# A fused attention and expert kernel: the first expert's second layer as eight block products, small maxima in PSUM, and a new order

## The chip, the cores and the metric

The kernel runs on one core of one Trainium2 chip. A core has a matrix engine (TensorE, PE in the profile), a vector engine (VectorE, DVE), an activation engine (ScalarE, ACT), a third elementwise engine (GpSimd, POOL) and an engine that starts transfers (SyncE, SP). The engines run side by side, each through its own list of instructions in order, and wait for one another by semaphores. SBUF is the on-chip memory that all of them reach; PSUM holds the results of matmuls in banks of 512 fp32 columns. The metric is the device time of one execution in microseconds (us): the median of three runs of the kernel before is 576.9 us, the lowest 575.75, the highest 577.33.

## What is computed

Three parts follow each other. Attention of 2 batches x 8 heads over 576 positions (half of the heads see the last 32 positions, half every 32nd position); a layer h = max(x w1, x w2, x w3) w_out over the 1152 tokens; and four experts, each of two layers, summed with a weight for each token:

```python
for e in range(E):                       # E = 4
    h = np.maximum(x @ w1[e], 0.0)       # 1152 x 512 by 512 x 1024
    out += p[:, e:e + 1] * (h @ w2[e])   # 1152 x 1024 by 1024 x 512
```

All is fp32. The kernel gets that precision on TensorE from f16 pairs: every operand is scaled by a power of two and split into a high part hi (a rounding to f16) and a rest lo (what is left), and each product is three matmuls, hi hi, hi lo and lo hi.

## The kernel before

The tokens are worked in quarters i = 0 to 3 (256 tokens for i = 0, 2 and 320 for i = 1, 3). In the attention part, `att_a` makes the scores of one pair of heads in PSUM, takes the largest of each row (L315), subtracts it and exponentiates on ScalarE; `att_n` divides by the row sums; `att_t` transposes on TensorE and `att_p` multiplies with v and splits the result into the tile `x` (high part L404 on ScalarE, rest L405 on VectorE). The next product in the same bank `ops` waits until L405 has read the last one. Where SUB holds an 'o', the maximum is not subtracted but goes, times 0.125 (L319, a VectorE operation on 3 to 5 columns), as a bias into the exponential. Meanwhile the six blocks of w1, w2, w3 come in (`load_w`), are decoded (`decode64`: L200 to L216), scaled (`scale_w`) and split (`split_w`: L441 to L448). A scale needs the maximum over all partitions: `all_max` makes it with a small matmul into the tile `rows` and a VectorE reduction (L135), and `scale_of` turns it into a power of two with three more tiny VectorE operations (L146, L149, L140). `g1` (L410 to L412) is the first layer with its three-way maximum on VectorE (L467, L468), its high part on ScalarE (L469) and its rest on GpSimd (L470); `g2` is the w_out layer.

In the experts both layers are products of 2x2 blocks by the seven-product scheme: instead of eight block products, seven, of sums and differences of blocks. So `prep_w1` and `prep_w2` load the weights, take a scale (eight ScalarE passes, L164, `junk`), and split not only the four blocks but also three sums of them (`splits`: sums L577 to L582, high parts L171, rests L172). In `gemm1`, seven products of a unit leave PSUM through ScalarE copies (L662, L666, L670, L680 to L685) and VectorE additions (L673, L676, L679) into the tiles `c`; `finish` makes three more sums of the hidden blocks in `hsum` (a part of the tile `x2acc`; four additions, L692, L693, L699, L700) and splits two blocks and the three sums (L703 high parts on ScalarE, L704 rests). `gemm2` then makes seven products of 12 matmuls (L817) for each of four units of an expert, and adds each product into one or two quarters of the output with the token's weight (L847, for the first expert's first write of a quarter L845 on ScalarE); `gemm2_tail` does the last 128 tokens with four plain products. Matmuls wait for a free bank: five banks `w` and three banks `mm` (`e`), freed by these copies and additions.

The order: ORDER lists the steps up to the first expert by hand; the tables A0 to C1 say how many steps of weight preparation go with each unit of the experts; LATE and a scheduler that sorts by priority set the order inside an engine. The strings SUB, ACC, REB, WLO, LOP, TW and others choose the engine of single steps (d VectorE, p GpSimd, a ScalarE).

Of the kernel before, what the change touches and what calls it, by code (L numbers as in the profile page):

```python
# [8 lines left out]
F32 = mybir.dt.float32  # L9
# [17 lines left out]
SUB = 'ddoppdpppoooodoo'  # L27
ACC = 'bggbggggggggbgbg'
SGN = 'dddpppdp'
PTC = 'aaaaaaaaaaaaaada'  # L30
LOW = 'adaadaaa'
REB = 'adppppda'
WLO = 'qddqdd'
ARS = 'dpdp'
RB = 1
QB = 3
XS = [0, 0, 10]
W20 = [5, 0, 5, 0, 1, 2, 1, 1]
W10 = [0, 2, 3, 0, 4, 2, 2, 2]
W2S = [0, 1, 1, 0, 1, 0, 6, 5, 6, 0, 6, 3, 7, 0, 0, 1, 0]  # L40
W1S = [10, 1, 1, 4, 0, 16, 6, 6, 5, 0, 2, 2, 2, 3, 2, 8, 0]

ORDER = """
    lw0 lq02 lq01 lv01 aa02 lq00 lq03 aa01 wd0 lq20 lv00 lw1 lq21 lv21 aa00 aa03 lv20 an02 lq23 aa20 an00 wa0
    an20 an03 wd1 lw2 vs0 lq22 wd2 at00 ap00 aa22 at02 lq12 lq10 at20 an01 lv10 at01 lv11 wp0 aa21 lq11 lq13
    at03 an22 aa23 an23 wa1 an21 vs2 ap02 at21 aa12 an12 aa11 ap01 an11 at22 lw3 wa3 lq30 wd3 lq32 aa10 lw4 wa2
    an10 at11 ap03 ap21 ap22 vs1 wd4 at23 ap20 ap23 lq33 wp2 aa13 lq31 at10 at12 lw5 wp1 wa4 g00 lv31 aa30 aa31
    an13 wp3 g01 ap10 g20 lv30 vs3 an30 at13 ap12 g22 wp4 g21 g02 ap11 lo0 aa32 aa33 g03 wa5 g23 od0 wd5 an32
    oa0 at32 ap13 g10 lo1 od1 ap32 an33 oa1 at30 wp5 os op3 at33 ap33 ap30 op1 g14 g25 an31 op4 g24 at31 ap31 fo
    ew ew ew op0 op5 op2 ew g04 g05 go20 go21 go22 go00 ew ew g11 go03 go23 ew go02 g15 go01 g12 xw ew g30 ew xw  # L50
    g13 g32 go10 xw ew g35 go11 ew g34 xw ew xw g31 g33 go30 ew ew ew xw xw cl xw ew go12 ew xw go31 go33 go32
    go13 fw fw fw m yw fw yw yw yw fw fw yw yw yw m m m yw fw fw yw
"""
CB = 5
LATE = [1, 4]
A0 = [9, 4, 0, 0, 11, 4, 3, 15]
A1 = [5, 10, 6, 2, 2, 6, 1, 3]
B0 = [0, 4, 0, 3, 1, 6, 5, 4, 4, 7, 0, 0, 0]
B1 = [3, 0, 2, 0, 0, 0, 0, 1, 5, 7, 0, 4, 0]
C1 = [8, 10, 4, 0, 7, 2, 2, 0, 9, 2, 0, 0, 0]  # L60
LOP = 'pddpdpdddpdddddddddddddd'
SOP = 'dpdddddd'
TW = 'ddddddpd'
TW0 = 'dddd'
TLO = 'd'
WHI = 'aaadap'
# [6 lines left out]
def kernel(ctx, tc, qk0l, qk0s, qk1l, qk1s, vl, vs0, vs1, vn, masks, w123, wo, probs, we1, we2, out):  # L73
# [39 lines left out]
    def rows_tile():  # L113
        if "psw" in lay:
            return lay["psw"].tile([128, 512], F32, tag="w", name=nm("rows"))[:, :128]
        return psa.tile([128, 512], F32, tag="t", name=nm("rows"))[:, :128]
# [963 lines left out]
```

## Time and profile before

| what | value |
|---|---|
| median of the runs | 576.9 us (575.75 to 577.33) |
| the profiled execution | 576.31 us, of it 574.5 us span |
| TensorE busy | 542.7 us, 94% |
| VectorE busy | 445.0 us, 77% |
| ScalarE busy | 351.2 us, 61% |
| GpSimd busy | 126.7 us, 22% |
| matmuls | 4633 |

The span runs from the first to the last instruction; 1.8 us of the profiled execution lie around it. TensorE is busy nearly all the time after the first 80 us, so the time is its columns plus its waits, and a wait is found in the rows that name what ended an idle time (`<-` stands before the releaser). A matmul's row lasts longer than the distance to the next one, because matmuls overlap: an idle time in the rows is thus shorter than the time lost.

### The profile page before, as it was taken

The page shows a single profiled execution, that of the slowest core. Times are in us where ns is not written, and L with a number is a line of the kernel's source. Part 1 is how long each engine was busy: PE and PEld are TensorE (multiplying, and loading weights), DVE is VectorE, ACT ScalarE, POOL GpSimd, SP SyncE. Part 2 cuts the span into 40 slices and gives each one's busy share as a digit, 9 for nine tenths or more (in the row PEclk, how much of TensorE's full clock was granted, in tenths as well). Part 3 has the DMA queues.
Part 4 walks back from the last instruction along what each step waited for, and adds up shares of the span by engine and source line. Part 5 has one row for each costly group of instructions (what it writes and reads, how often), then busy time and mean ns, then how long its engine had stood idle before and what let it go on. Part 6 is the DMA issues. An engine that isn't in the chain of part 4 may idle for free.

```text
span 574.5 us, 11609 instructions
## 1 busy us (share of the span) xinstructions
PE 542.7 (94%) x4633; PEld 444.5 (77%) x4633; DVE 445.0 (77%) x835; ACT 351.2 (61%) x798; POOL 126.7 (22%) x108
## 2 busy tenths in 40 slices
PE   7779989999999999988999989999999999999997
PEld 4668768788777778766788867888767888867886
DVE  3999999752269524899998789899779999989732
ACT  3578556554446254998969888438697444776300
POOL 0467773710112112401020040010040010040000
PEclk9969999999999999999999999999999999999999
DMA  8998514124004000200425501444500331101342
GB/s 309 341 391 263 174 41 149 52 74 148 1 1 148 2 0 1 75 2 19 147 65 211 166 2 38 127 120 158 185 1 19 103 118 57 38 1 37 94 129 74
DMA packets 24150, 58.60 MB, mean 102 GB/s; under 512 B 3272, under 2 KB 3528, under 8 KB 23328
## 3 DMA queue, kind: packets, MB, share of 16 engines
q1 hardware_dynamic: 23952, 57.57, 30.7%
q8 instruction: 36, 0.59, 0.4%
q10 hardware_dynamic: 144, 0.30, 0.2%
q14 instruction: 18, 0.15, 0.1%
HBM read 48.42 MB, written 9.44 MB: 101 GB/s over the span
## 4 chain that ended last, share of the span: by engine, by line
PE 47%; DVE 19%; ACT 13%; DMA 10%; issue 10%; POOL 1%; SPq 0%; ACTq 0%; POOLq 0%; DVEq 0%
PE g L410 7%; PE g L412 7%; PE g L411 7%; PE e L817 7%; PE w L817 5%; DMA st<-in_we_dram 5%; ACT junk L164 3%; DMA v<-in_vs_dram 2%; DVE w1ops L172 2%; PE e L651 2%; PE e L653 2%; PE e L652 2%; ACT hb L703 2%; PE w L651 2%; PE ops L397 2%
## 5 line engine op out<-in xcount | busy, mean ns | idle before, releaser
L817 PEld LDWEIGHTS <-hb 128*128 128x128 f16 x1008 | 98.2, 98 | 17.3 <-issue 5.3
L410 PE MATMUL g<-x,w 128*128 128x256 f16 (+1 forms) x288 | 80.8, 287 | 3.1 <-DVE t L467 1.9
L412 PE MATMUL g<-x,w 128*128 128x256 f16 (+1 forms) x288 | 82.3, 287 | 0.0
L411 PE MATMUL g<-x,w 128*128 128x256 f16 (+1 forms) x288 | 82.3, 287 | 0.0
L651 PE MATMUL e<-xops,w1ops 128*128 128x320 f16 (+1 forms) x224 | 63.6, 287 | 6.4 <-ACT c L662 2.4
L651 PE MATMUL w<-xops,w1ops 128*128 128x256 f16 (+1 forms) x224 | 63.3, 284 | 2.6 <-ACT c L666 1.3
L652 PE MATMUL e<-xops,w1ops 128*128 128x320 f16 (+1 forms) x224 | 63.9, 287 | 0.0
L652 PE MATMUL w<-xops,w1ops 128*128 128x256 f16 (+1 forms) x224 | 63.5, 284 | 0.0
L653 PE MATMUL w<-xops,w1ops 128*128 128x256 f16 (+1 forms) x224 | 63.3, 284 | 0.0
L653 PE MATMUL e<-xops,w1ops 128*128 128x320 f16 (+1 forms) x224 | 63.2, 288 | 0.0
L652 PEld LDWEIGHTS <-w1ops 128*128 128x128 f16 x448 | 43.8, 98 | 22.9 <-issue 12.3
L653 PEld LDWEIGHTS <-w1ops 128*128 128x128 f16 x448 | 43.8, 98 | 10.9
L651 PEld LDWEIGHTS <-w1ops 128*128 128x128 f16 x448 | 43.8, 98 | 10.5
L470 POOL TENSOR_TENSOR h<-t,h 128x256 f16<-128x256 f32 (+1 forms) x24 | 21.7, 910 | 88.0 <-ACT h L469 82.2
L817 PE MATMUL e<-B,hb 128*128 128x256 f16 x288 | 35.0, 272 | 1.7 <-ACT c L684 1.6
L411 PEld LDWEIGHTS <-w 128*128 128x128 f16 x288 | 28.3, 98 | 9.9 <-issue 2.8
L410 PEld LDWEIGHTS <-w 128*128 128x128 f16 x288 | 28.3, 98 | 8.5 <-issue 0.9
L412 PEld LDWEIGHTS <-w 128*128 128x128 f16 x288 | 28.3, 98 | 7.2
L703 ACT CAST hb<-c 128x512 f16<-128x512 f32 x40 | 24.5, 620 | 12.2 <-DVE c L699 11.5
L704 DVE TENSOR_TENSOR hb<-x2acc,hb 128x768 f16<-128x768 f32 (+1 forms) x31 | 27.9, 904 | 4.5 <-ACT hb L703 4.3
L171 ACT ACTIVATE w1ops<-st,s 128x1024 f16<-128x1024 f32 x19 | 21.2, 1141 | 15.8 <-DVE st L582 5.5
L580 POOL TENSOR_TENSOR st<-st,x2acc 128x1024 f32<-128x1024 f32 x3 | 8.9, 2976 | 93.4 <-DVE x2acc L578 63.5
(229 smaller groups left out, 1383.8 us busy)
## 6 DMA issues: line engine op xcount, KB each, us to landing
st<-in_we_dram SPq DMA_DIRECT2D x10, 1024.0 KB, 5.5
st<-in_w_dram SPq DMA_DIRECT2D x6, 1536.0 KB, 8.0
c<-accd SPq DMA_DIRECT2D x24, 256.0 KB, 2.8
accd<-c SPq DMA_DIRECT2D x23, 256.0 KB, 2.0
st<-in_wo_dram SPq DMA_DIRECT2D x2, 1536.0 KB, 7.7
st<-in_we_dram SPq DMA_DIRECT2D x6, 512.0 KB, 4.5
x2acc<-in_we_dram SPq DMA_DIRECT2D x6, 512.0 KB, 4.1
qk<-in_qk1s_dram SPq DMA_DIRECT2D x4, 684.0 KB, 9.7
```

The costliest lines, as they stand in the source:

```text
L164: nc.scalar.activation(junk, src, AF.Abs, scale=2.0**-12, accum_out=dst)
L171: nc.scalar.activation(hi, src, AF.Copy, scale=s)
L410: nc.tensor.matmul(psum, lh, rh, start=i == 0, stop=False)
L411: nc.tensor.matmul(psum, lh, rl, start=False, stop=False)
L412: nc.tensor.matmul(psum, ll, rh, start=False, stop=i == n - 1)
L470: nc.gpsimd.tensor_tensor(hh[:, 1, fc, :], t1[:, :n], hh[:, 0, fc, :], ALU.subtract)
L651: nc.tensor.matmul(pt, wh, xh, start=first and k == 0, stop=False, skip_group_check=True)
L652: nc.tensor.matmul(pt, wh, xl, start=False, stop=False, skip_group_check=True)
L653: nc.tensor.matmul(pt, wl, xh, start=False, stop=k == 1, skip_group_check=True)
L703: nc.scalar.copy(hi, src)
L704: eng(LOP[8 * g + 4 * j + fp]).tensor_tensor(lo, src, hi, ALU.subtract)
L817: nc.tensor.matmul(pt, hop[:, x, f, sl], wop[:, y, f, :], start=start and n == 0, stop=n == 11, skip_group_check=True)
```

## The change

It does six things. First, for expert 0 alone the second layer is done with eight plain block products in place of seven: `finish` skips the sums of hidden blocks and splits two blocks instead of five, `prep_w2` splits the four weight blocks as they are, and `gemm2` accumulates each output quarter over two products in one bank and writes it out with a single ScalarE instruction. Second, the tile `rows` is kept whole and its columns 128 and 129 hold the maximum and the scale before rounding, so these small values lie in PSUM, not SBUF. Third, where SUB is 'o' the row maxima are written into columns 500 on of the score bank in PSUM, and L319's successor (L318) reads them there. Fourth, other engines: the small addition `ars` of quarters 1 and 2 goes to ScalarE, six of the 24 rests of `g1` from GpSimd to VectorE (HLO), two multiplications of the decoding from GpSimd to VectorE (REB), the split of block 5 of w1, w2, w3 to GpSimd (WLO), one sum of w2's blocks per later expert from GpSimd to VectorE (TW, at L580), one rest of the hidden blocks as well (LOP). Fifth, one more head pair subtracts its maximum (SUB), and three row sums change sides (ACC). Sixth, ORDER, A0 to C1 and LATE are new.

```diff
-SUB = 'ddoppdpppoooodoo'
-ACC = 'bggbggggggggbgbg'
+SUB = 'ddoppdpppoooodod'
+ACC = 'bgbbgggggbggbggg'
...
-REB = 'adppppda'
-WLO = 'qddqdd'
-ARS = 'dpdp'
+REB = 'addppdda'
+WLO = 'qddqdq'
+ARS = 'daad'
...
-    lw0 lq02 lq01 lv01 aa02 lq00 lq03 aa01 wd0 lq20 lv00 lw1 lq21 lv21 aa00 aa03 lv20 an02 lq23 aa20 an00 wa0
+    lw0 lq02 lq01 lv01 aa02 lq00 lq03 lq20 aa01 aa00 lq21 lv00 an02 aa03 lw1 wd0 wa0 wp0 lv20 lq23 lw2 lv21 wd1
...
-LATE = [1, 4]
-A0 = [9, 4, 0, 0, 11, 4, 3, 15]
+HLO = 'pdpdpppppppdpdpppdppppdp'
+LATE = [0, 0]
+A0 = [18, 12, 2, 0, 11, 2, 6, 14]
...
-LOP = 'pddpdpdddpdddddddddddddd'
+LOP = 'pddpdpdddddddddddddddddd'
-TW = 'ddddddpd'
+TW = 'dddddddd'
...
-            return lay["psw"].tile([128, 512], F32, tag="w", name=nm("rows"))[:, :128]
+            return lay["psw"].tile([128, 512], F32, tag="w", name=nm("rows"))
...
-        allr = sc.tile([128, 1], F32, tag="allr", name=nm("allr"))
-        nc.vector.tensor_reduce(allr, rows, AX.X, ALU.max)
+        allr, m = rows[:, 128:129], rows[:, 129:130]
+        nc.vector.tensor_reduce(allr, rows[:, :128], AX.X, ALU.max)
...
-            nc.vector.tensor_reduce(mx[:rows, gs], s3, AX.X, ALU.max, negate=True)
+            top_of = st[:rows, 500 : 500 + n] if SUB[4 * i + p] == "o" else mx[:rows, gs]
+            nc.vector.tensor_reduce(top_of, s3, AX.X, ALU.max, negate=True)
...
-                nc.vector.tensor_scalar(mx[:rows, gs], mx[:rows, gs], 0.125, None, ALU.mult)
+                nc.vector.tensor_scalar(mx[:rows, gs], top_of, 0.125, None, ALU.mult)
...
-        if ARS[i] == "p":
+        if ARS[i] == "a":
+            nc.scalar.activation(rs[:rows, :ng], sm[:rows, :ng], AF.Copy, bias=1e-9)
+        elif ARS[i] == "p":
...
-        nc.gpsimd.tensor_tensor(hh[:, 1, fc, :], t1[:, :n], hh[:, 0, fc, :], ALU.subtract)
+        eng(HLO[6 * i + fc]).tensor_tensor(hh[:, 1, fc, :], t1[:, :n], hh[:, 0, fc, :], ALU.subtract)
...
+        if e == 0:
+            for n, x in zip((1, 3, 2, 5), blocks):
+                yield from split1(op[n][:, 0], op[n][:, 1], x, s)
+            return
...
-                add(s[:, 0], m[1][:, 0], m[1][:, 1], ALU.add)
-                add(s[:, 1], s[:, 0], m[0][:, 0], ALU.subtract)
+                if e:
+                    add(s[:, 0], m[1][:, 0], m[1][:, 1], ALU.add)
+                    add(s[:, 1], s[:, 0], m[0][:, 0], ALU.subtract)
...
-                for g, (t, src) in enumerate(zip(hh, (m[0], m[1], s))):
+                for g, (t, src) in enumerate(zip(hh, (m[0], m[1], s) if e else m)):
...
+        if e == 0:
+
+            def part(b, z):
+                pt = bank(z == 1)
+                for n, (x, y) in enumerate(((1, (1, 3)), (2, (2, 5))) if b == 0 else ((3, (1, 3)), (6, (2, 5)))):
+                    mult(pt, h[x], w[y[z]], sl, n == 0, n == 1)
+                nc.scalar.activation(o[b][:, Z[z]], pt, AF.Copy, scale=k[b])
+                if z:
+                    nc.sync.dma_start(out=accd[:, 2 * j + q, 512 * b : 512 * b + 512], in_=o[b])
```

Three places show what moved. The first is VectorE's list at the first quarter's tile `x` (here `x_130`; `sps` are score banks, `amx` row maxima, `st` a weight block in decoding). Before:

```order
L315 TENSOR_REDUCE amx_323<-sps_325 128x4
...
L315 TENSOR_REDUCE amx_376<-sps_378 128x4
L319 TENSOR_SCALAR amx_323<-amx_323 128x4
L405 SCALAR_TENSOR_TENSOR x_130<-ops_311,s_295,x_130 128x256
L319 TENSOR_SCALAR amx_376<-amx_376 128x4
L216 SCALAR_TENSOR_TENSOR r_277<-st_1_72 128x1536
```

After the change, at the same place:

```order
L314 TENSOR_REDUCE sps_342<-sps_342 128x4
L126 TENSOR_REDUCE red_479<-vm_475 128x1
L318 TENSOR_SCALAR amx_340<-sps_342 128x4
L411 SCALAR_TENSOR_TENSOR x_130<-ops_328,s_282,x_130 128x256
L318 TENSOR_SCALAR amx_387<-sps_389 128x4
L214 SCALAR_TENSOR_TENSOR r_251<-st_1_72 128x1536
```

The sequence is the same, but the small multiplication takes its input from the score bank. The second place is VectorE's list some 35 us later, at a head pair of quarter 2 (`x_132` its tile, `h` the rests of `g1`). Before:

```order
L202 TENSOR_SCALAR st_0_71<-st_0_71 128x1536
L135 TENSOR_REDUCE allr_654<-rows_652 128x1
...
L315 TENSOR_REDUCE amx_830<-sps_832 128x5
L319 TENSOR_SCALAR amx_812<-amx_812 128x5
L149 TENSOR_SCALAR inv_657<-m_649 128x1
L329 TENSOR_TENSOR p_829<-sps_832,amx_830 128x480
```

After the change:

```order
L200 TENSOR_SCALAR st_0_71<-st_0_71 128x1536
L355 RECIPROCAL ar_915<-ars_913 120x6
L476 TENSOR_TENSOR h_713<-t_831,h_713 128x256
L314 TENSOR_REDUCE sps_766<-sps_766 128x5
L131 TENSOR_REDUCE rows_656<-rows_656 128x1
L318 TENSOR_SCALAR amx_764<-sps_766 128x5
L411 SCALAR_TENSOR_TENSOR x_132<-ops_679,s_487,x_132 128x256
```

A rest of `g1` (L476, both inputs in SBUF) now stands between the decoding step and the small multiplication. The third place is ScalarE's list where the first expert's second weights are split (`B` and `B2c` hold them; `e` and `w` are banks of the first layer). Before:

```order
L666 COPY c_2544<-w_3134 128x320
L171 ACTIVATE B_3093<-st_0_71,s_3091 128x1024
L171 ACTIVATE B2c<-st_1_72,s_3091 128x1024
L171 ACTIVATE B_3093<-st_1_72,s_3091 128x1024
L697 CAST tailh<-c_2545 128x2x64
L703 CAST hb_2534<-c_2545 128x2x256
L684 ACTIVATE c_2546<-e_2981 128x320
...
L171 ACTIVATE B2c<-st_0_71,s_3091 128x1024
```

After the change:

```order
L692 ACTIVATE c_2627<-e_2931 128x320
L169 ACTIVATE B_3035<-st_0_71,s_3033 128x1024
L169 ACTIVATE B_3036<-st_0_71,s_3033 128x1024
L169 ACTIVATE B_3035<-st_1_72,s_3033 128x1024
L169 ACTIVATE B2c<-st_1_72,s_3033 128x1024
L693 ACTIVATE x2acc<-x2acc 128x640
```

All four remaining splits stand in one row; before, three stood together and four more followed singly.

## Rows read from the trace of the kernel before

**Rows 1.** Page: busy tenths of TensorE in 40 slices of 14.4 us.

```profile
PE   7779989999999999988999989999999999999997
```

**Rows 2.** Stretches: busy us (instructions) of each engine, clock, DMA share, GB/s.

```profile
5.00:80.00 75.00, 61.53 (x510) 51.56 (x509) 64.69 (x116) 45.31 (x153) 44.22 (x29) 0.93 0.80 272
...
225.00:345.00 120.00, 112.40 (x942) 91.44 (x940) 106.66 (x194) 104.27 (x230) 21.97 (x16) 1.00 0.25 82
345.00:574.40 229.40, 220.30 (x1906) 185.95 (x1903) 190.82 (x363) 127.02 (x256) 22.66 (x19) 1.00 0.27 81
```

**Rows 3.** TensorE's waits, 5 to 80 us: us in total, times, longest.

```profile
PE sps L308 <- DMA mk<-in_masks_dram: 2.8, 1, 2.8
PE ops L397 <- issue: 2.5, 1, 2.5
PE g L410 <- DVE t L467: 1.9, 1, 1.9
...
PE sps L308 <- DVE p L329: 1.3, 2, 1.0
```

**Rows 4.** Time line of VectorE and GpSimd, 28 to 36 us: start, duration, instruction.

```profile
29.75 2.63 DVE L319 TENSOR_SCALAR amx<-amx 128x4 f32<-128x4 f32 x1
32.30 0.47 DVE L405 SCALAR_TENSOR_TENSOR x<-ops,s,x 128x256 f16<-128x256 f32 x1
29.27 3.09 POOL L448 TENSOR_TENSOR w<-r,w 128x1536 f16<-128x1536 f32 x1 [1.59 <-DVE ar L354]
```

**Rows 5.** The same engines, 63 to 80 us.

```profile
75.75 3.14 DVE L319 TENSOR_SCALAR amx<-amx 120x3 f32<-120x3 f32 x1
75.26 3.60 POOL L207 TENSOR_SCALAR st<-st 128x1536 bf16<-128x1536 f32 x1
```

**Rows 6.** All of L319: durations min/median/max in ns.

```profile
L319 DVE TENSOR_SCALAR amx<-amx x9: 153/1309/4041, 15.3 to 98.6; 128x4 f32<-128x4 f32 x4, 120x3 f32<-120x3 f32 x4, 128x5 f32<-128x5 f32 x1
```

**Rows 7.** A stretch at the low clock, columns as in rows 2.

```profile
27.00:38.00 11.00, 8.16 (x52) 6.96 (x52) 10.75 (x20) 7.11 (x16) 8.07 (x6) 0.53 1.01 398
```

**Rows 8.** Chain that ended last, second layer of the last expert: start, us.

```profile
545.47 2.62 PE w L817 x24
```

**Rows 9.** Groups by shape: busy us, mean ns | idle before.

```profile
L704 DVE TENSOR_TENSOR hb<-x2acc,hb 128x768 f16<-128x768 f32 x24 | 23.3, 969 | 4.5 <-ACT hb L703 4.3
L703 ACT CAST hb<-x2acc 128x768 f16<-128x768 f32 x24 | 20.0, 832 | 1.8 <-DVE x2acc L700 1.7
L692 DVE TENSOR_TENSOR x2acc<-c 128x256 f32<-128x256 f32 x23 | 10.5, 457 | 1.4 <-ACT c L684 1.3
L172 DVE SCALAR_TENSOR_TENSOR B2c<-st,s,B2c 128x1024 f16<-128x1024 f32 x6 | 7.7, 1278 | 0.0
L577 DVE TENSOR_TENSOR st<-st 128x1024 f32<-128x1024 f32 x4 | 4.9, 1220 | 0.0
L847 DVE SCALAR_TENSOR_TENSOR c<-e,coef,c 128x256 f32<-128x256 f32 x46 | 21.8, 480 | 8.3 <-PE e L817 7.3 <-DMA c<-accd 1.0
```

**Rows 10.** TensorE's waits, 225 to 345 us: the first two groups.

```profile
PE e L817 <- ACT c L684: 1.6, 2, 1.2
PE e L651 <- ACT c L670: 1.0, 1, 1.0
```

**Rows 11.** Time line: a split on ScalarE, and TensorE's wait behind it.

```profile
255.22 1.19 ACT L171 ACTIVATE B2c<-st,s 128x1024 f16<-128x1024 f32 x1
257.15 0.30 PE L651 MATMUL e<-xops,w1ops 128*128 128x320 f16 x1 [0.94 <-DVE c L676]
```

**Rows 12.** Time line, 376 to 384 us: VectorE's rest and GpSimd's sum.

```profile
379.88 3.27 DVE L172 SCALAR_TENSOR_TENSOR w1ops<-x2acc,s,w1ops 128x1024 f16<-128x1024 f32 x1
379.70 2.36 POOL L580 TENSOR_TENSOR st<-st,x2acc 128x1024 f32<-128x1024 f32 x1 [32.05 <-DVE x2acc L578]
```

**Rows 13.** TensorE's waits, 345 us to the end: the first two groups.

```profile
PE e L651 <- ACT c L662: 1.5, 2, 1.2
PE w L651 <- ACT c L666: 1.3, 1, 1.3
```

More of the change, by code (lines that the diff above doesn't have):

```diff
@@ L114, in rows_tile @@
         if "psw" in lay:
-            return lay["psw"].tile([128, 512], F32, tag="w", name=nm("rows"))[:, :128]
-        return psa.tile([128, 512], F32, tag="t", name=nm("rows"))[:, :128]
+            return lay["psw"].tile([128, 512], F32, tag="w", name=nm("rows"))
+        return psa.tile([128, 512], F32, tag="t", name=nm("rows"))
     uid = [0]
@@ L132, in all_max @@
         rows = rows_tile()
-        nc.tensor.matmul(rows, red.to_broadcast([128, 128]), eye, start=True, stop=True)
-        allr = sc.tile([128, 1], F32, tag="allr", name=nm("allr"))
-        nc.vector.tensor_reduce(allr, rows, AX.X, ALU.max)
-        return allr
+        nc.tensor.matmul(rows[:, :128], red.to_broadcast([128, 128]), eye, start=True, stop=True)
+        allr, m = rows[:, 128:129], rows[:, 129:130]
+        nc.vector.tensor_reduce(allr, rows[:, :128], AX.X, ALU.max)
+        return allr, m
     def finish_scale(inv):
@@ L354, in att_n @@
         nc.vector.reciprocal(r[:rows, :ng], rs[:rows, :ng])
-        nc.gpsimd.tensor_tensor(p3, p3, r[:rows, :ng].unsqueeze(2).to_broadcast([rows, ng, nk]), ALU.mult)
+        if NRM[4 * i + p] == "a":
+            for g in range(ng):
+                nc.scalar.activation(p3[:, g], p3[:, g], AF.Copy, scale=r[:rows, g : g + 1])
+        else:
+            rb = r[:rows, :ng].unsqueeze(2).to_broadcast([rows, ng, nk])
+            eng(NRM[4 * i + p]).tensor_tensor(p3, p3, rb, ALU.mult)
     def att_t(i, p):
@@ L625, in prep_w2 @@
         blocks = [pcs[k][:, :, 256 * z : 256 * z + 256] for k in range(2) for z in range(2)]
-        yield from splits(TW if e else TW0, blocks, lambda n: (op[n][:, 0], op[n][:, 1]), s)
+        if e == 0:
+            for n, x in zip((1, 3, 2, 5), blocks):
+                yield from split1(op[n][:, 0], op[n][:, 1], x, s)
+            return
+        yield from splits(TW, blocks, lambda n: (op[n][:, 0], op[n][:, 1]), s)
     OPS = {1: 0, 2: 1, 3: 2, 6: 3, 4: 4, 0: 5, 5: 6}
@@ L817, in mult @@
                 nc.tensor.matmul(
-                    pt, hop[:, x, f, sl], wop[:, y, f, :], start=start and n == 0, stop=n == 11, skip_group_check=True
+                    pt, hop[:, x, f, sl], wop[:, y, f, :], start=start and n == 0, stop=stop and n == 11, skip_group_check=True
                 )
@@ L840, in gemm2, with first, to @@
         mul = lambda n, pt, start=True: mult(pt, h[n], w[n], sl, start)
-        def to(b, z, pt, first=False):
+        if e == 0:
[6 more added lines that the diff above has]
+                    nc.sync.dma_start(out=accd[:, 2 * j + q, 512 * b : 512 * b + 512], in_=o[b])
+            def first():
+                o.extend(total(e, 2 * j + q, 2))
+                part(0, 0)
+            none = lambda: None
+            return first, lambda: part(0, 1), none, lambda: part(1, 0), none, lambda: part(1, 1), none, none
+        def to(b, z, pt):
             x = o[b][:, Z[z]]
-            if first and e == 0:
-                nc.scalar.activation(x, pt, AF.Copy, scale=k[b])
-            else:
-                nc.vector.scalar_tensor_tensor(x, pt, k[b], x, ALU.mult, ALU.add)
+            nc.vector.scalar_tensor_tensor(x, pt, k[b], x, ALU.mult, ALU.add)
         def p1():
```

67 lines of the change are left out of this document (32 added, 35 removed).

## The prediction

> **What bounds the kernel now.** I read the page's slices of busy time first: TensorE is at 9 tenths or more from the sixth slice on with few exceptions, and below that in the first five [rows 1]. So the time is TensorE's columns plus its waits, and a change is worth what it does to these two. The stretches give the sizes [rows 2]: from 5 to 80 us TensorE idles 75.0 - 61.5 = 13.5 us, from 225 to 345 us (the first expert and the start of the second) 7.6 us, from 345 us to the end 9.1 us, of which the last 4 us are the final write after the last matmul. Then I asked in each stretch who ended the waits. Early, 2.8 us are the arrival of the mask, and three groups come from VectorE: 2.5 us before a product with v, 1.9 us before a matmul of the first layer, 1.3 us in two pieces before new scores [rows 3]. From 225 to 345 us there are twelve waits, 7.1 us together, nearly all for a bank that ScalarE or VectorE has not yet emptied [rows 10]. From 345 us there are seven of the same kind, 5.1 us together [rows 13]. A wait costs a little more than its row, since a matmul's row goes on beside the next one: 0.30 us for 320 columns [rows 11], where by pace 24 matmuls of 256 columns take 2.62 us [rows 8], so 0.109 us each and 0.136 us for 320 columns. I add 0.16 us to each wait. The twelve are then 9.0 us; with the idle time that the rows leave unnamed (7.6 against 7.1) I count 9.5 us.
>
> **What TensorE gets to do.** Four units of the first expert's second layer go from seven products to eight, each of 12 matmuls: 48 more at 0.109 us [rows 8] make +5.2 us. TensorE is the engine that sets the end in that stretch, so this is paid in full unless the waits shrink. The tail of 128 tokens had four products and keeps four.
>
> **What VectorE and ScalarE lose in that stretch.** Eight hidden units lose the rest of the three sums, 0.97 us each, and their high parts on ScalarE, 0.83 us each; 28 of 32 additions stood on VectorE at about 0.46 us; the weights lose three splits (rest 1.28 us) and four sums (1.22 us); the second layer loses 13 accumulations at 0.48 us [rows 9]. VectorE: 7.8 + 12.9 + 3.8 + 4.9 + 6.2 = 35.6 us less, of 106.7 us busy in 120 [rows 2]. Two things come back from GpSimd, one rest and one sum for the second expert, together about 2 us. ScalarE: 6.7 us of high parts and three splits of nearly 1.2 us [rows 11], so 10 us less of 104.3 us [rows 2]; writing the plain products out costs it what the first writes cost before, 16 instructions for 16.
>
> So VectorE falls from the engine that is nearly full to one with a quarter free, and ScalarE stays the busiest of the two. What is late next is ScalarE: the four splits that remain stand in one row in its list, between two copies that free banks. Before, a row of three such splits ended with a wait of 0.94 us on TensorE [rows 11], 1.1 us with its tail; for four I take 1.5 us. I leave another 1.4 us for waits at the first units, which have nothing to do with the sums: 2.9 of 9.5 us stay. **This stretch: -6.6 + 5.2 = -1.4 us.** Bounds: -4.3 us if no wait is left, +5.2 us if all stay.
>
> **The early stretch.** The rows of the small multiplication L319 are the surprise of this profile: the same instruction on 3 to 5 columns takes 153 ns at best, 1309 ns in the median and 4041 ns at worst [rows 6]. The long ones lie under a long GpSimd operation and end with it: begun at 29.75 us, 2.63 us long, it ends at 32.38 us, and GpSimd's rest of a weight block ends at 32.36 us [rows 4]; begun at 75.75 us it ends at 78.89 us, and GpSimd's operation at 78.86 us [rows 5]. Behind the first stands L405, which frees the bank `ops`, and TensorE waits 2.5 us there; behind the second stands the maximum of `g1`, and TensorE waits 1.9 us [rows 3]. Nine such instructions take 13.9 us together. The change reads the operand from PSUM. The Trainium skill, "SBUF — State Buffer", section Who interferes with whom, says that VectorE and GpSimd share a pair of SBUF ports, which a two-port instruction holds to its end, and "VectorE: DVE Perf Modes", section Why PSUM operands drop a tier, that an operand in PSUM rules the two-port mode out; by that rule these waits end, and the rows above agree as far as they go, though none here shows the PSUM form.
>
> From the rows alone the new form is bounded by 153 ns (no wait) and by 4041 ns (the wait stays, if place and not operand makes it); I take the first, since the ends coincide to 0.03 us in both pairs. Of the three VectorE groups, 2.5 + 1.9 + 1.0 (the longer of the last) = 5.4 us, 5.9 us with the tails, I keep 2.1 us: at 30 us the next matmuls need GpSimd's rest of block 0 as well, which lands at 32.36 us now [rows 4] and stands behind one more small GpSimd operation after the change, so half of that wait stays (1.2 us); and 0.9 us for a delay that moves on. **-3.8 us.** The maxima in `rows` are now held in a bank through three more tiny operations; transposes use the same pair of banks. I cost that at nothing: at the place where it bites first, TensorE waits for a load anyway. If that cover is gone, it is the length of the decoding steps between, up to 3 us.
>
> A lower bound for this stretch: from 27 to 38 us the granted clock is 0.53, that is half speed nearly throughout, with TensorE busy for 8.2 us [rows 7]. If the shorter waits before it kept the clock at full, that work would take about half, 3.8 us less. I don't count on it, since the loads that leave gaps before 27 us are the same. The other edits here (six rests and two multiplications to VectorE, the additions `ars` to ScalarE, one head pair that subtracts) shift some 5 us between engines that gain more than that; at nothing.
>
> **The later experts.** GpSimd's one sum of weight blocks per expert takes 2.36 us, and a VectorE rest that meets it takes 3.27 us in place of about 1.28 [rows 12, 9]. On VectorE the sum costs 1.22 us [rows 9] and the meeting ends: three times about 0.8 us saved on VectorE and a shorter chain for ScalarE. Of the 5.1 us of waits there I take a quarter off: **-1.2 us**, between -3 and +2, as the tables of steps and LATE are new and could put preparation ahead of a copy that frees a bank.
>
> **The sum.** -1.4 - 3.8 - 1.2 = -6.4 us on the profiled execution of 576.3 us: 569.9 us. The median of the runs lies 0.6 us above that execution, so 570.5 us.
>
> **Rivals.** (a) The port wait moves on. In VectorE's new list a rest of `g1` with both inputs in SBUF stands right behind a decoding step, where GpSimd's 3.6 us operation follows; if that rest waits as L319 did, all behind it waits too, and the early gain is nil: 570.5 + 3.8 = 574.3 us. Against it speaks that at the two places above the operation behind is one that reads a bank. The same section of the Trainium skill's page "SBUF — State Buffer" says that an instruction with two SBUF inputs does collide with a GpSimd instruction that reads SBUF; rows 12 agree, where such a rest took 3.27 us beside GpSimd's sum. (b) Slower: the eight products are paid and the waits stay. If ScalarE's row of four splits and its in-order copies, not VectorE's sums, hold the banks (most rows of that stretch name ScalarE [rows 10]), then 9.5 us of waits stay at 8 and more, the stretch costs +3.7 or more, and with half the early gain and none later the time is 576.9 + 3.7 - 1.9 = 578.7 us. It decides from 6.9 us of waits left on, where the saving no longer covers 5.2 us and the early gain has to. (c) More: the clock stays up early (-3.8 us) and the waits at 225 to 345 us go to 1.5 us: 570.5 - 3.8 - 1.4 = 565.3 us, and less with the later experts' 3 us. (d) The new order of the first 80 us makes a new wait of about the size of the ones removed, for a load or a transposing bank: 574 to 577 us.
>
> **How the numbers follow.** The forecast (566.5 to 573.5 us) gets 0.50, (a) 0.13, (b) 0.13, (c) 0.14, (d) 0.10. The range leaves out the lower half of (c) and the upper half of (b): 563.0 to 578.0 us. About 0.3%, 1.7 us, is what a measurement of this kernel can tell from no change, so faster means under 575.2 us: the forecast, (c), most of (a), a third of (d), 0.77; same 0.11; slower 0.12.
>
> **What would show it.** In the profile after: L318 at 0.15 to 0.3 us throughout (the step on the port); no wait of 1.9 us before the first layer near 75 us, and the wait near 30 us halved; VectorE busy for some 72 us of the 120 us that now hold 106.7; TensorE's waits from the first expert's second layer to the second expert's first layer at 3 us. I would be wrong if L476 or a decoding step showed durations of 2 us and more under a GpSimd operation with TensorE waiting behind, if the row of four splits were followed by waits well over 1.5 us, or if new waits for loads stood in the first 80 us.

## The result, and the profile after

The changed kernel takes 563.25 us (562.95 to 564.82), the kernel before beside it 577.0 us: a ratio of 0.977, with an interval of 0.975 to 0.979. The gain is 13.7 us (12.7 by all eight runs, below), where 6.4 us were forecast. The sign was right and the early gain came about as forecast; the gains of the first expert and behind it were far larger than forecast. One kernel below, a_late, turned out to be the same program: in the two traces the instructions of every engine come in the same order. Its four runs took 563.7 to 568.4 us, so the changed program's eight runs have a median of 564.3 us. A loss that is given below against 563.25 us is 1 us smaller against all eight (in brackets where that matters).

The page of the changed kernel: TensorE, slices of 14.1 us, and the chain that ended last.

```profile
PE 544.6 (97%) x4681; PEld 450.3 (80%) x4681; DVE 410.6 (73%) x794; ACT 345.4 (62%) x794; POOL 101.0 (18%) x82
...
PE   7899999999999999999999999999889999999997
...
DVE  3979989662459424779564789898888999878832
...
PEclk7679999999999999999999999999999999999999
...
PE 84%; DMA 6%; DVE 4%; ACT 4%; POOL 1%; issue 0%; SPq 0%; DVEq 0%; ACTq 0%
```

TensorE runs 48 matmuls more and is busy for nearly the same time, yet 97% of the span; against [rows 1] the eights between 80 and 345 us are gone, and two stand later. The chain consists of TensorE alone for 84%. The stretches, columns as in [rows 2]:

```profile
5.00:80.00 75.00, 67.22 (x561) 56.52 (x560) 64.47 (x128) 49.98 (x165) 44.53 (x24) 0.84 0.83 275
225.00:345.00 120.00, 119.79 (x1021) 99.61 (x1020) 87.78 (x155) 101.92 (x234) 10.15 (x9) 1.00 0.26 84
345.00:561.40 216.40, 208.79 (x1822) 177.81 (x1819) 176.43 (x341) 117.09 (x232) 14.71 (x14) 1.00 0.27 85
```

From 225 to 345 us TensorE idles 0.2 us where it idled 7.6, and VectorE is busy for 87.8 us where it was 106.7. From 5 to 80 us it idles 7.8 us in place of 13.5. TensorE's waits after (us in total, times, longest) are, from 5 to 80 us, then the only one from 220 to 340 us, then all from 345 us on:

```profile
PE sps L306 <- DMA mk<-in_masks_dram: 3.0, 1, 3.0
PE sps L306 <- ACT p L334: 1.2, 1, 1.2
PE ops L403 <- DVE x L411: 0.9, 1, 0.9
...
PE w L659 <- ACT c L674: 0.2, 1, 0.2
...
PE e L659 <- ACT c L670: 1.5, 1, 1.5
PE e L659 <- DVE c L684: 1.1, 1, 1.1
PE w L659 <- DVE c L687: 0.6, 1, 0.6
PE e L659 <- ACT c L692: 0.3, 1, 0.3
```

Of the early groups of [rows 3] the mask stays; the 2.5 us before `ops` near 30 us and the 1.9 us before the first layer are gone. The 0.9 us before `ops` are a new wait in another place, at 64.5 us: L411, which frees that bank, stands there behind a rest L476 of 1.67 us (rows below). The twelve waits whose largest stand in [rows 10] have shrunk to one. What is left late stands at 400 to 414 us, in the third expert's first layer, 3.5 us in four waits, where the seven waits from 345 us on were 5.1 us.

To see where each kernel wins or loses, this table takes from each trace the start of the last matmul of the w_out layer and of each expert's second layer (us from the span's start). The last column is the median of the runs. Each row is one execution, and its first column can differ by up to 4.7 us between executions with the same order of early instructions. With before's early lists (before, b_eight, b8_dv, b8_ds) it is 221.8 to 223.5, the middle 222.1; with the maxima in PSUM under the old order (b_psum, b_both, a_earlyold) 218.8 to 219.6, the middle 218.9; with the new early lists (changed, a_late, a_tw, a_latesold, a_seven) 216.4 to 221.1, the middle 217.9.

| kernel | w_out layer | expert 1 | expert 2 | expert 3 | expert 4 | median |
|---|---|---|---|---|---|---|
| before | 222.0 | 312.3 | 400.0 | 485.9 | 570.1 | 577.0 |
| changed | 216.9 | 304.0 | 387.2 | 476.9 | 557.1 | 563.3 |
| b_eight | 221.8 | 308.9 | 392.7 | 480.8 | 562.7 | 569.2 |
| b_psum | 219.6 | 309.6 | 399.4 | 486.6 | 570.4 | 577.0 |
| b_both | 218.8 | 305.9 | 389.5 | 477.9 | 561.0 | 568.6 |
| b8_dv | 222.2 | 311.8 | 401.6 | 490.2 | 572.6 | 579.4 |
| b8_ds | 223.5 | 312.4 | 395.9 | 484.9 | 567.3 | 573.8 |
| a_seven | 217.9 | 307.2 | 393.3 | 482.9 | 563.8 | 569.9 |
| a_latesold | 216.4 | 303.5 | 386.8 | 476.0 | 559.4 | 565.9 |
| a_tw | 218.2 | 305.3 | 389.4 | 478.0 | 561.2 | 566.4 |
| a_late | 221.1 | 308.2 | 392.1 | 482.1 | 562.2 | 565.6 |
| a_earlyold | 218.9 | 306.1 | 390.2 | 478.9 | 559.0 | 566.3 |
| a_eng | 220.7 | 307.2 | 390.4 | 479.8 | 560.8 | 567.0 |
| a_topsbuf | 219.7 | 306.8 | 390.0 | 479.9 | 560.0 | 566.4 |
| a_rowsbuf | 227.8 | 314.9 | 398.1 | 487.7 | 567.9 | 571.6 |
| a_sbufmax | 226.3 | 313.4 | 397.2 | 487.1 | 567.3 | 572.1 |

The changed kernel's trace gains 5.1 us before the experts, 3.2 us in the first expert, 4.5 us in the second and 0.2 us behind it. By the middles of the groups the early gain is 4.2 us, of it 3.2 us by the maxima in PSUM under the old order and some 1 us by the new order, which is no more than the spread.

### The profile page after: what moved, and what is told of

The parts are those of the page before. It is cut to its first block, busy times and chain, and to the rows that moved or that the text cites. A ratio compares the mean times of both kernels' runs of the same rounds, so it can differ in the third digit from the quotient of the medians.

```text
span 561.5 us, 11622 instructions
## 1 busy us (share of the span) xinstructions
PE 544.6 (97%) x4681; PEld 450.3 (80%) x4681; DVE 410.6 (73%) x794; ACT 345.4 (62%) x794; POOL 101.0 (18%) x82
## 4 chain that ended last, share of the span: by engine, by line
PE 84%; DMA 6%; DVE 4%; ACT 4%; POOL 1%; issue 0%; SPq 0%; DVEq 0%; ACTq 0%
PE e L827 15%; PE w L827 13%; PE g L416 9%; PE g L417 9%; PE g L418 8%; PE e L659 4%; PE e L660 4%; PE e L661 4%; PE w L659 4%; PE w L661 4%; PE w L660 4%; PE ops L403 2%; DMA st<-in_w_dram 2%; PE sps L309 2%; DMA mk<-in_masks_dram 1%; PE tps L373 1%
## 5 line engine op out<-in xcount | busy, mean ns | idle before, releaser
L827 PEld LDWEIGHTS <-hb 128*128 128x128 f16 x1056 | 103.1, 98 | 12.6
L476 POOL TENSOR_TENSOR h<-t,h 128x320 f16<-128x320 f32 (+1 forms) x18 | 16.4, 916 | 88.2 <-ACT h L475 88.2
L162 ACT ACTIVATE junk<-st 128x512 f16<-128x512 f32 x44 | 27.8, 631 | 5.6 <-DMA st<-in_we_dram 4.7
L827 PE MATMUL w<-B,hb 128*128 128x256 f16 x240 | 29.4, 273 | 0.0
L827 PE MATMUL e<-B,hb 128*128 128x256 f16 x240 | 29.1, 273 | 0.0
L714 POOL TENSOR_TENSOR hb<-c,hb 128x512 f16<-128x512 f32 x7 | 9.0, 1279 | 108.7 <-ACT hb L713 99.8
```

Of the source, the lines that this page charges most:

```text
L162: nc.scalar.activation(junk, src, AF.Abs, scale=2.0**-12, accum_out=dst)
L476: eng(HLO[6 * i + fc]).tensor_tensor(hh[:, 1, fc, :], t1[:, :n], hh[:, 0, fc, :], ALU.subtract)
L827: nc.tensor.matmul(pt, hop[:, x, f, sl], wop[:, y, f, :], start=start and n == 0, stop=stop and n == 11, skip_group_check=True)
```

## Experiments on the first expert

**The eight products alone, and taken out of the change.** b_eight puts them into the kernel before, with all its tables; a_seven takes them out of the changed kernel.

```diff
 # b_eight (the kernel before)
-        yield from splits(TW if e else TW0, blocks, lambda n: (op[n][:, 0], op[n][:, 1]), s)
+        if e == 0:
+            for n, x in zip((1, 3, 2, 5), blocks):
+                yield from split1(op[n][:, 0], op[n][:, 1], x, s)
+            return
+        yield from splits(TW, blocks, lambda n: (op[n][:, 0], op[n][:, 1]), s)
...
 # a_seven (the changed kernel): the same lines the other way, with 'dddd' for expert 0
```

> The kernel before (577.0 us) with the first expert's second layer by eight products and nothing else; all tables of steps and engines as before. Theory 1 (the products themselves): the work that VectorE and ScalarE lose empties TensorE's banks in time; with the old lists the stretch of the first expert and the start of the second gains 3 to 5 us net of the 5.2 us for 48 more matmuls, and the time is 572 to 574 us. Theory 2 (the lists): the waits go only because the new lists also put splits and decoding elsewhere; with the old lists the waits stay in good part and the 5.2 us are paid: 576 to 580 us.

> The changed kernel (563.3 us) with the first expert's second layer by seven products again, its rests on VectorE, all else as in the change. Theory 1 (the products): VectorE is full again between 217 and 304 us, the waits of some 6 us there come back, less 5.2 us for the matmuls saved, and the second expert's preparation is late again, so that part of the 4.7 us of the later experts goes too: 567 to 571 us. Theory 2 (the lists): 48 matmuls fewer and hardly a wait more: 559 to 563 us, and this would be the better kernel.

b_eight takes 569.2 us beside 576.1 us, a ratio of 0.987 (0.986 to 0.989): 6.9 us. a_seven takes 569.9 us, 6.6 us more than the changed kernel (5.6). So with old lists and new the eight products are worth some 6 to 7 us net of their own 5.2 us, and the lists are not what makes them work. The table says where: b_eight gains 3.2 us up to the end of the first expert and 4.0 us in the second, where nothing was edited.

How the second expert gains shows in the chains, from 300 us on (start us, us, what); first the kernel before:

```profile
308.19 1.28 DVE hb L172
309.47 1.14 DVE st L577
310.91 1.27 DVE hb L172
...
317.73 5.13 DMA st<-in_we_dram
322.88 0.72 ACT junk L164 x2
...
324.43 0.61 ACT junk L164 x2
```

then b_eight:

```profile
301.82 1.14 DVE st L582
302.95 1.20 DVE hb L172
304.17 1.30 DVE hb L172
305.49 6.76 DMA st<-in_we_dram
...
312.86 0.19 ACT junk L164
313.05 0.27 ACT c L670
```

VectorE's rests and sums of the second expert's weights free the buffers `st`; only then does the next load start; behind it come ScalarE's passes over the new weights, in one list with the copies `c` that free TensorE's banks. With VectorE relieved, the load starts at 305.5 us, 3.4 us before the first expert ends, and not at 317.7 us, 5.4 us behind that end. The passes stand among the copies of the next units in both kernels. In b_eight the last is done by 315.6 us and TensorE waits 0.3 us there; in the kernel before they run from 322.9 to 334.6 us, and TensorE's waits from 330 to 338 us beside them cost 2.6 us. Another 1.4 us were lost at 385.8 and 398.8 us behind VectorE's additions, so the chain of the load is the larger part of the 4.0 us, not all of it. (These costs are by the distances between matmuls, see the account of the prediction.)

**Which engine's relief.** Two kernels give a part of the lost work back to b_eight, into tiles that nobody reads.

```diff
 # b8_dv: the four additions for expert 0 again, and
+                if e == 0:
+                    nc.vector.tensor_tensor(hh[2][:, :, 1, fp], s, xops[j][:, 0:3, 0, 0, :256], ALU.subtract)
 # b8_ds
+                if e == 0:
+                    nc.scalar.copy(hh[2][:, :, 0, fp], xops[j][:, 0:3, 0, 0, :256])
```

> The kernel before with the eight products (569.2 us), and VectorE made to do again, into tiles that nobody reads, what the first expert's hidden units lost on it: the additions of the sums and the rest of the third part, 12.9 + 7.8 = 20.7 us by the prediction's own sum. The output is the reference's; the work added is of no use. Theory V (VectorE's load is what held the banks): most of the 7 us come back, 573 to 576 us. Theory S (ScalarE's high parts and splits in one row held them): within 1.5 us of 569.2. Theory N (neither load, but the weights' and the second layer's own shorter chains): within 1.5 us as well, and the same for ScalarE's load.

> The kernel before with the eight products (569.2 us), and ScalarE made to do again, into tiles that nobody reads, eight copies of the size of the high parts that it lost (0.83 us each, 6.7 us). The output is the reference's. Theory S (ScalarE, the busiest of the two after the change, decides): 571.5 to 574 us. Theory V (VectorE): within 1 us of 569.2. If both this kernel and the one with VectorE's load stay near 569.2, theory N.

b8_dv takes 579.4 us, 10.2 us more; b8_ds 573.8 us, 4.6 us more (10.0 and 4.1 by the ratios, as the kernel before took 577.1 us beside them). So both theories hold in part: a microsecond on VectorE costs about half of one (10.2 of the 20.5 us that it is busier in the trace; four of the additions went to GpSimd), one on ScalarE about 0.7 (4.1 to 4.6 of the 6.1 us that its eight copies take). In b8_dv TensorE's wait stands right behind that chain; its two largest groups of waits from 222 to 402 us:

```profile
PE e L655 <- ACT c L666: 4.5, 1, 4.5
PE w L655 <- ACT c L674: 1.7, 1, 1.7
```

ScalarE's list there, where it idled 2.64 us for the load and has passes over it ahead of the copy L666 that frees the bank:

```profile
316.24 0.63 ACT L164 ACTIVATE junk<-st 128x512 f16<-128x512 f32 x1 [2.64 <-DMA st<-in_we_dram]
...
318.59 0.36 ACT L666 COPY c<-e 128x256 f32<-128x256 f32 x1
```

and the stretches around the wait:

```profile
312.00:318.00 6.00, 2.22 (x19) 1.68 (x18) 2.54 (x3) 3.24 (x8) 0.00 (x0) 1.00 0.82 241
318.00:324.00 6.00, 5.00 (x33) 3.87 (x33) 0.78 (x3) 5.56 (x19) 0.00 (x0) 0.72 0.51 196
```

Its load of `st` starts at 310.9 us, and VectorE itself idles by then: what is late is not VectorE's queue but what hung on its earlier work. After the wait the granted clock is 0.72 over 6 us, so the lower of its two levels (1.2 and 2.4 GHz) for a good part of it, and that comes on top of the wait: 1.4 us by the distances between matmuls. The cost exceeds the whole gain of b_eight by 3.3 us. The clock is a part of this; that the rest is the 5.2 us of columns, which stay paid while the waits came back, is argued and not shown.

## Experiments on the maxima in PSUM

**Alone, and with the eight products.**

```diff
 # b_psum and b_both (the kernel before; b_both with the eight products too)
-        allr = sc.tile([128, 1], F32, tag="allr", name=nm("allr"))
-        nc.vector.tensor_reduce(allr, rows, AX.X, ALU.max)
+        allr, m = rows[:, 128:129], rows[:, 129:130]
+        nc.vector.tensor_reduce(allr, rows[:, :128], AX.X, ALU.max)
...
+            top_of = st[:rows, 500 : 500 + n] if SUB[4 * i + p] == "o" else mx[:rows, gs]
```

> The kernel before (577.0 us) with the small maxima and their products in PSUM and nothing else. Theory 1 (the port): the waits of the small multiplication under GpSimd's long operations end, L318's rows stand at 0.15 us, and the first 80 us lose 3 to 4 us: 573 to 574 us. Theory 2 (the early order): the 5.1 us that the change gains up to the end of the last layer before the experts come from the new order of the first 80 us, and the old order only trades one wait for another: 576 to 577 us, with L318's rows short all the same.

> The kernel before with the eight products and the maxima in PSUM, all tables and orders as before. If the two edits make the gain, some 566 to 569 us (their two gains added, 4 and 5 us, and a little of the later experts' 4.7 us); if the lists make it, 574 us or more, and the 11 us to the changed kernel's 563.3 are the lists' own.

b_psum takes 577.0 us beside 576.1, a ratio of 1.002 (1.000 to 1.004): nothing. b_both takes 568.6 us, 0.6 us less than b_eight. Yet the small multiplication did what was forecast; it is L320 in b_psum (durations min/median/max in ns):

```profile
L320 DVE TENSOR_SCALAR amx<-sps x9: 145/151/163, 15.9 to 82.3; 128x4 f32<-128x4 f32 x4, 120x3 f32<-120x3 f32 x4, 128x5 f32<-128x5 f32 x1
```

and L318 in the changed kernel:

```profile
L318 DVE TENSOR_SCALAR amx<-sps x7: 147/149/163, 14.9 to 77.7; 128x4 f32<-128x4 f32 x4, 120x3 f32<-120x3 f32 x2, 128x5 f32<-128x5 f32 x1
```

against 153 to 4041 ns in [rows 6]. The table shows the give-back: b_psum is 2.4 us ahead at the end of the w_out layer and 2.7 us at the end of the first expert, and loses all but 0.6 us in the second. There the chain of buffer, load and passes stands as before: its load starts at 313.1 us, 3.5 us behind the first expert's end. b_both stays some 3 us ahead of b_eight through the third expert and loses 1.2 us of them in the fourth; its traced execution is also its fastest, 1.2 us under its median.

**One kind of maximum back at a time.** In the changed kernel, a_topsbuf puts the scores' maxima (L318's) back into SBUF, a_rowsbuf those of the scales, a_sbufmax both.

```diff
 # a_topsbuf
-            top_of = st[:rows, 500 : 500 + n] if SUB[4 * i + p] == "o" else mx[:rows, gs]
+            top_of = mx[:rows, gs]
 # a_rowsbuf
-        allr, m = rows[:, 128:129], rows[:, 129:130]
+        allr = sc.tile([128, 1], F32, tag="allr", name=nm("allr"))
...
+        m = sc.tile([128, 1], F32, tag="m", name=nm("m"))
```

> The changed kernel (563.3 us) with the small maxima and their products in SBUF again, all else as changed. Theory 1 (the port waits still cost under the new order): the early stretch loses the 2 to 3 us that the maxima in PSUM gave in the trace with the old order, the later stretches are no longer limited by VectorE and keep the loss, so 565.5 to 567 us. Theory 2 (the new order had put other work beside GpSimd's long operations): 563 to 564 us, with long rows of the small multiplication all the same.

> The changed kernel (563.3 us) with only the maxima of the scores and their small multiplication (L318) back in SBUF; the maxima of the scales stay in PSUM. Both kinds back in SBUF gave 572.1 us. Theory 1 (the rows that the prediction priced, L318's, carry the loss): 569 to 572 us. Theory 2 (the three tiny steps of the scales, which the prediction costed at nothing, carry it, since TensorE's longest new wait there, 4.4 us, was put down to such a step): 563 to 566 us.

> The changed kernel (563.3 us) with only the maxima of the scales and their products back in SBUF; the maxima of the scores stay in PSUM. Theory 1 (L318's rows carry the loss of 8.8 us): 563 to 566 us. Theory 2 (the scales' steps carry it): 569 to 572 us. If both this kernel and the one with L318 back lie near 567, the two share the loss.

a_sbufmax loses 8.8 us, a_topsbuf 3.2, a_rowsbuf 8.4 (7.8, 2.1 and 7.3); in the traces all of it before the experts, and nothing is given back later. The first column of a_topsbuf lies within the spread of the new lists, those of the other two do not. In a_topsbuf the old pattern is there again, with a wait of 1.4 us on TensorE before `ops` at 32.4 us: the worst L318 and GpSimd's operation beside it (start, us) end 0.03 us apart, at 31.97 and 31.94 us.

```profile
29.83 2.14 DVE L318 TENSOR_SCALAR amx<-amx 128x4 f32<-128x4 f32 x1
...
28.14 3.80 POOL L454 TENSOR_TENSOR w<-r,w 128x1536 f16<-128x1536 f32 x1
```

In a_rowsbuf the tiny steps themselves are as short as ever (135 to 156 ns for the multiplication L142). What differs is the list: the scheduler lays VectorE's steps in another order. Time line around its longest wait, first the changed kernel:

```profile
61.54 1.67 DVE L476 TENSOR_TENSOR h<-t,h 128x256 f16<-128x256 f32 x1
63.13 0.65 DVE L314 TENSOR_REDUCE sps<-sps 128x5 f32<-128x480 f32 x1
63.70 0.28 DVE L131 TENSOR_REDUCE rows<-rows 128x1 f32<-128x128 f32 x1
63.97 0.47 DVE L411 SCALAR_TENSOR_TENSOR x<-ops,s,x 128x256 f16<-128x256 f32 x1
64.92 0.15 DVE L142 TENSOR_SCALAR rows<-rows 128x1 f32<-128x1 f32 x1
```

then a_rowsbuf:

```profile
63.49 5.13 POOL L205 TENSOR_SCALAR st<-st 128x1536 bf16<-128x1536 f32 x1 [2.85 <-DVE st L200]
...
65.63 2.99 DVE L476 TENSOR_TENSOR h<-t,h 128x256 f16<-128x256 f32 x1
...
69.18 2.60 DVE L214 SCALAR_TENSOR_TENSOR r<-st 128x1536 int32<-128x1536 int32 x1
71.71 0.14 DVE L142 TENSOR_SCALAR m<-allr 128x1 f32<-128x1 f32 x1
...
72.40 0.47 DVE L411 SCALAR_TENSOR_TENSOR x<-ops,s,x 128x256 f16<-128x256 f32 x1
72.80 0.14 DVE L145 TENSOR_SCALAR inv<-m 128x1 int32<-128x1 int32 x1
...
72.93 0.37 PE L403 MATMUL ops<-pt,v 64*64 64x64 f32 x2 [4.15 <-DVE inv L145]
```

The rest L476 waits for GpSimd (it ends at 68.62 us, GpSimd's operation at 68.62), a decoding step of 2.60 us comes next, and only then L411, which frees `ops` (the row names L145, which ends 0.07 us later beside it): TensorE waits 4.15 us. In the changed kernel L411 stands 0.3 us behind the reduction L131. The granted clock then is 0.50 from 71.7 to 78.5 us, the lower level, where the changed kernel is at 1.00; with TensorE busy for 5.57 us of it, that is an estimated 2.8 us more. a_sbufmax shows the same: a wait of 4.4 us, 0.51 from 69.2 to 76.1 us, an estimated 2.1 us. So their loss is the waits that the list makes and the clock behind them. The Trainium skill, "SBUF — State Buffer", section Who interferes with whom, says that a VectorE instruction with two SBUF inputs contends with a GpSimd instruction that reads SBUF; L476 has two such inputs, and the trace agrees, with 2.99 us in place of the 0.41 us that the same line takes at best.

So the new order and the maxima in PSUM are not two gains to be added: without the maxima (a_sbufmax, 226.3 us at the end of the w_out layer) the new order is slower than the old one, by 4.3 us in the traces, of which some 1.4 us are that a_sbufmax's traced execution was its slowest. And none of these three undoes a tile's place alone, since the lists change with it. Why the scheduler moves these steps when two small tiles change place was not tried.

## Experiments on the lists and engines

a_latesold has before's late tables in the changed kernel, a_tw and a_late one of them each; a_earlyold has before's early order and engines, a_eng the engines alone.

```diff
 # a_tw
-TW = 'dddddddd'
+TW = 'ddddddpd'
 # a_late
-LATE = [0, 0]
+LATE = [1, 4]
 # a_eng
-REB = 'addppdda'
+REB = 'adppppda'
-ARS = 'daad'
+ARS = 'dpdp'
-HLO = 'pdpdpppppppdpdpppdppppdp'
+HLO = 'pppppppppppppppppppppppp'
 # a_latesold: LATE, A0 to C1, LOP and TW of before
 # a_earlyold: ORDER, SUB, ACC, PTC, REB, WLO, ARS, WHI of before, HLO as in a_eng
```

> The changed kernel (563.3 us) with the late tables of before (steps of preparation per unit, the distance of late work, the engine of the weight blocks' sums and of one rest); its early order and early engines as changed. With before's order and engines throughout, the two other edits gave 568.6 us. Theory L (the late tables and the sum on VectorE carry the rest of the gain, as the trace gives 1.4 us lost after the second expert with the old ones and none with the new): 566 to 568 us. Theory O (the new early order carries it): 563 to 565 us.

> The changed kernel (563.3 us) with the one sum of weight blocks per expert on GpSimd again (three sums). Theory 1 (the prediction's step: the sum on VectorE and the end of its meeting with a rest give 1.2 us or more): 564.5 to 566 us. Theory 2 (the tables of steps carry what the late lists gave, 2.6 us, and the sum's place is hidden): within 1 us of 563.3.

> The changed kernel (563.3 us) with before's two distances of late work (1 for the hidden units' splits, 4 for the preparation of weights) and nothing else. Theory 1 (the distances carry the late lists' 2.6 us): 565 to 566.5 us. Theory 2 (they do nothing by themselves): within 1 us of 563.3.

a_latesold loses 2.6 us and a_tw 3.2 us (1.6 and 2.1), so GpSimd's sum, the one table that a_tw changes, seems as dear as all late lists together; but a_tw's runs (566.1 to 567.4 us) lie within those of a_late, which is the changed program. TensorE's waits from 218 us to the end in a_tw are 5.4 us, where the changed kernel's, shown above, are 3.7:

```profile
PE e L659 <- ACT c L670: 2.2, 3, 1.1
PE e L827 <- DVE c L871: 1.8, 2, 1.2
PE e L659 <- ACT x2acc L670: 0.8, 1, 0.8
PE w L659 <- ACT c L674: 0.6, 2, 0.4
```

The waits before a second layer (L827), which the changed kernel lacks, are new. Do the late lists give something by themselves? Two pairs answer. a_latesold and the changed kernel have the same early lists: 2.6 us (1.6). b_both and a_earlyold have the same early lists too, the old ones with the maxima in PSUM, and differ in the late tables alone: 568.6 us (567.4 to 568.8) against 566.3 (565.5 to 567.1), 2.3 us (2.6 by the ratios), and their runs do not overlap. So with the maxima in PSUM the new late lists give some 2.3 us under either early order; how much of it is GpSimd's sum, a_tw does not settle. By the distances between matmuls, kernels with the old late lists lose more behind the w_out layer the earlier that stretch begins: 5.8 us from 221.8 us on (b_eight), 7.2 from 218.8 (b_both), 8.3 from 216.4 (a_latesold). With the new ones it is 4.9 us from 218.9 on (a_earlyold), 5.5 from 216.9 (changed) and 6.4 from 221.1 (a_late). The new late lists without the maxima in PSUM were not tried.

a_late has LATE of before, yet it is the changed program once more, so LATE does nothing here, and its 2.3 us are no loss. The two traces show what one program can vary by: 4.3 us at the end of the w_out layer. In a_late's, the transfers came later, and from 65 to 75 us the granted clock was 0.83, where the other has 1.00.

> The changed kernel (563.3 us) with before's early order and early engines; the late tables as changed. Theory L: 564 to 565.5 us, only the 1.9 us that the two traces differ in by the end of the last early layer are lost. Theory O: 567 to 569 us, no better than the two edits with all of before's lists (568.6 us). A third case: the early gain is taken back later, since the loads of the third expert's weights set its start: 563 us, nothing lost.

> The changed kernel (563.3 us) with before's engines for all rests of the early layer's blocks, for the two rebuilding steps and for the additions before the reciprocals, and with the new order. Theory 1 (the order carries the 1.9 us by which the early stretch is shorter than with the two other edits alone; the prediction costed the engines at nothing): within 1 us of 563.3. Theory 2 (the six rests and two multiplications taken from GpSimd carry it, since GpSimd's operations are what VectorE waits for): 565 to 566 us.

a_earlyold loses 3.1 us (2.0), 2.1 of them before the experts; a_eng loses 3.7 us (2.7; 566.8 to 568.2). In the traces most of a_eng's loss is early, but its first column (220.7) lies within the spread of the new lists. So the edits that the prediction costed at nothing, rests and multiplications moved from GpSimd to VectorE and the additions `ars` to ScalarE, are worth some 3 us in the new order; that they and the order were worth the same can't be told from these runs, and the new order under the old engines is an order that nobody would choose. No kernel here beats the changed one.

In steps, the way from before to after is: 577.0 us, with the eight products 569.2, with the maxima in PSUM too 568.6, with the new late lists 566.3 (a_earlyold), with the early order and engines 563.3.

## Why the prediction was right in sign and wrong in size

**The waits of the first expert, mis-sized.** The sum gave -1.4 us: 9.5 us of waits, 2.9 kept, 5.2 paid. Measured alone it is -6.9 us. The mechanism held: VectorE and ScalarE were relieved, the waits went, and the 5.2 us were paid. Two terms were too small. First the base, 9.5 us: the waits that VectorE's load causes were counted up to 345 us and the rest booked as the later experts' own. By the distance from each matmul's start to the next, less 0.1088 us for each 256 columns (nearly the pace of [rows 8]), TensorE loses 8.5 us in the first expert's stretch and 4.2 us in the second's, 12.7 in all. Second, what stays: 1.0 us in b_eight, 0.8 in the changed kernel, not 2.9. 12.7 - 1.0 - 5.2 = 6.5 us explains b_eight. (With the 0.1092 us of [rows 8] the losses are 12.0 and 0.3 us, and the difference is the same.) The row of four splits on ScalarE, for which 1.5 us were kept, cost no wait in the changed kernel [rows 11 had 0.94 for three]. VectorE's busy time fell less than the sum of the lost rows, 35.6 us: in b_eight the lost rows add up to 35.8 us, but they overlap, and the busy time of the trace fell by 28.9 us. That the changed kernel is busy for 87.8 us, not 72, in those 120 us is also because it does 79 more matmuls in them.

**ScalarE next.** That ScalarE is late next was right: its microsecond costs more than VectorE's. But it was already the partner in the old waits, and relieving both ended them. Where eight copies were put back on ScalarE (b8_ds), its row of four splits (250.5 to 254.9 us) was followed by a wait of 2.25 us on TensorE.

**The early stretch.** -3.8 us was forecast; -5.1 us is what the one pair of traces shows, -4.2 us the middles of the groups. The term held. The step on L319 was right, with its price: 0.15 us throughout, and some 2 to 3 us lost when it is undone (of 5.9, 2.1 were kept). The split of the term was not: the wait near 30 us, of which half was to stay, is gone, and 0.9 us stand at 64.5 us; that the sum came so close is in part luck. "At nothing" was wrong for the maxima in `rows`, which cost 7 to 8 us if undone in the new order, by way of the list and the clock, and for the engines of rests and multiplications (some 3 us).

**The later experts.** -1.2 us was forecast for the late edits, the sum on GpSimd above all, "between -3 and +2". With the maxima in PSUM the new late lists give 2.3 us (b_both against a_earlyold), so the term was about half of what came. Most of what the traces gain from the second expert on (4.7 us) is another thing: b_eight has 4.1 us of it without any late edit. That a rest which meets the sum [rows 12] is the mechanism was not shown apart from the longer chain.

The parts now add up: 6.9 + 2.3 + 4.2 = 13.4 us, where 13.7 were measured. What failed is thus the size of the first expert's term above all (5.5 of the 7.3 us that the forecast lacked), and that of the later experts' next.

**The clock.** The lower bound hoped for a full clock from 27 to 38 us [rows 7]. It fell: the changed kernel is at 0.66, 0.66 and 0.57 in these three stretches, and the early gain came all the same.

```profile
5.00:15.00 10.00, 7.00 (x34) 6.31 (x32) 4.95 (x5) 3.18 (x2) 0.00 (x0) 0.66 1.04 355
15.00:26.00 11.00, 9.14 (x41) 6.87 (x41) 10.61 (x31) 5.96 (x27) 4.37 (x3) 0.66 1.01 323
26.00:37.00 11.00, 10.10 (x73) 8.36 (x74) 9.62 (x18) 8.65 (x23) 10.12 (x5) 0.57 1.01 414
```

**The rivals.** (b), that the eight products are paid and the waits stay, fell with b_eight. (c) was right on the waits (under 1.5 us) and wrong on the clock. Its point of decision, "from 6.9 us of waits left on", does not follow from its numbers: 9.5 - 5.2 = 4.3 us is where the saving no longer covers the columns. (a) came in small in the changed kernel: L476 took 1.67 us at 61.5 us, with 0.9 us of waiting before `ops` behind it. At 100.27 us it took 2.76 us and ended with a GpSimd operation (L205, 99.39 + 3.64 us), and TensorE did not wait. In a_rowsbuf (a) and (d) are both there, where the rest waits for GpSimd and the list holds `ops`. b_psum shows the trap that the prediction missed: an early gain can be lost in a stretch that another chain limits. With the eight products alone it is hardly let through either (b_both, 0.6 us); with the new late lists too it is (a_earlyold, 2.9 us under b_eight).

## What to carry to other kernels

When an engine that is nearly full is relieved, look for its effect one stage further: follow what its work frees (a buffer, the load behind it, the passes over that load) and count the waits of that stage too. Where a scheduler sets the lists, an edit of a tile's place can change them all, so it is not free: undo it alone, in the new list and in the old, before calling it hidden. Gains in different stretches add up only if the later stretch is not held by a chain of its own. Before an undo of 2 or 3 us is given a meaning, measure the unchanged program once more: here two sets of runs of one program lay 2.3 us apart.

## What the runs showed of the hardware

TensorE's granted clock fell behind waits in the middle of its work. A 4.5 us wait in b8_dv was followed by 0.72 over 6 us, the waits of 4.15 us in a_rowsbuf and 4.4 us in a_sbufmax by 0.50 and 0.51 over 7 us, a 2.2 us wait in a_seven at 412.9 us by 0.50 from 413.8 to 417.2 us. In a_late, waits of 1.0, 0.4 and 1.4 us within 62 to 67 us were followed by 0.51 from 67.5 to 71.0 us. The kernel before, with waits of 1.2 us at most from 225 to 345 us, is at 1.00 throughout that stretch [rows 2].

The small multiplications on VectorE took 145 to 163 ns once their operand lay in PSUM, whatever GpSimd did; with it in SBUF the same ones took up to 4041 ns [rows 6], and that longest one lasted through two GpSimd operations in a row. The end of the w_out layer varied by 4.3 us between two executions of the same program.
